# Window attention and two MLPs on one Trainium2 core: where layer two's pieces of x are formed, and in which banks the last half accumulates

## The chip, the core and the metric

One of the eight cores of a Trainium2 chip runs the whole program. Its engines work side by side, each through a queue of its own: TensorE (PE, its weight loads PEld) multiplies matrices, VectorE (DVE), ScalarE (ACT) and GpSimd (POOL) do the elementwise work, and SyncE (SP) issues the transfers (DMA). The metric is the device time of one execution in microseconds (us); less is better.

## The reference

Four sequences of 576 tokens, eight heads of 64, go through causal attention in a window of 64 tokens; the 2304 x 512 result goes through two MLPs with 2048 hidden units, the first with `s * relu(h)^2 + b`, the second with a leaky relu of its own slope for each unit.

```python
scores = scale * np.matmul(q, k.transpose(0, 1, 3, 2))
mask = (rel >= 0) & (rel < 64)
attn = softmax(np.where(mask, scores, -1e9))
x = np.matmul(attn, v)                                  # as 2304 x 512
r = np.maximum(x @ moe_w_in, 0.0)
x = (moe_s * (r * r) + moe_b) @ moe_w_out               # layer one
h = x @ moe2_w_in
out = (np.maximum(h, 0.0) + alpha * np.minimum(h, 0.0)) @ moe2_w_out   # layer two
```

## The kernel before

**Numbers in two parts.** Every operand of a large product is held as a high and a low part, hi + lo (`pair`, L667): hi is a cast (ScalarE, or VectorE at L671), lo the rest (a subtraction on VectorE, L674). A product is three matmuls: hi x hi, hi x lo, lo x hi.

**Tiling.** A hidden tile f is 128 of the 2048 hidden units; `GROUPS` splits the 16 tiles of a layer into groups whose projections are summed in PSUM, and the groups' sums are added up in AY in SBUF (`sums`, L1168). The first two groups of layer one work on blocks of tokens (`hidden`, L1058). All later groups take the tokens in three turns q of 768, each two halves c of 384 (`HALF`), and the hidden tiles in pairs. A pair by a turn is a 2 x 2 block product in seven products instead of eight (`hidden_pair`, L913; its matmuls are L939): seven combinations of x, the *pieces* 1 to 7, by seven of the weights, six matmuls of 384 columns each. With 48 matmuls of projections (`project`, L1096, at L1139) a pair by a turn is 90 matmuls. Layer two's groups have four tiles each, so two pairs: in each turn a piece is used twice.

**Banks of PSUM.** Products 1 and 5 begin in two banks of a ring of two (`b1`, `b4`, tag "h"), products 6, 7 and 3 run in the two halves of `hb`; ScalarE carries running sums from one to the next (L950: b1 to hb's first half, that to the second, that to b4), VectorE adds the product 5 to both halves of `hb` at once (L967). The hidden function's relus (L1035, L1036 in layer two, L1016 in layer one) read `b1`, `b4` and that sum; then come L1039, the cast to hi (L1004 on ScalarE, L1005 on VectorE) and the subtraction to lo (L1009). The projections accumulate in the four banks y0 to y3, one buffer each, over the tiles of a group; after a half's last tile VectorE adds each into AY (L1188; L1185 at the end of layer one; L1181 copies at the start of layer two), and the last group's sums go out (L1193).

**Pieces of x.** In layer two they are formed from AY by `x_pieces` (L869): pieces 1, 2 and 3 are blocks of x, 5, 6, 7 and 4 differences T1 to T4 (L882, two places in AS, each used twice a turn). `x_stage` puts hi and lo of a piece into AG with `staging` (L678), which has room for two pieces, and stores it in DRAM (`x_store`, L792). At a turn's start `x_load` (L901, its transfer L907) fetches the seven pieces into seven slots of XA; a slot is free when the second pair of the turn before has used it. A turn that follows itself at a group's boundary keeps its pieces. So layer two's first group loads three turns, the other three groups two each. `weight_pair` (L725) forms the weights' combinations for a pair ahead of time, through the same AG (L757) and DRAM; `weight_load` fetches them (L778). `weight` converts an output tile's weights (L639 to L674).

**Order of the work.** `T.step` registers a step with its possible engines, what it reads and writes, and a due time `at`; `T.emit` (L162) then plays all steps through with costs of its own and writes each engine's queue in that order: of the steps that can start first on an engine it takes the one with the earliest `at`. On the chip each queue runs in this order. `T.tile` and `T.place` make a step wait for the users of what it overwrites, in the order in which the steps were registered. `begin` holds when a turn should start, `PAIR` the planned time of a pair by a turn (15.4 us); products are due at begin + pair x `PAIR` + a seventh for each, a half's projections from 1.7 `PAIR` after begin on.

## Time and profile before

| | us |
|---|---|
| median of 3 runs | 862.49 (862.11 to 864.53) |
| the profiled execution | 862.62 |
| its span, first to last instruction | 860.9 |
| TensorE busy | 838.3 (97%) |
| VectorE busy | 650.4 (76%) |
| ScalarE busy | 511.2 (59%) |
| pieces loaded, `ax<-xd` | 112 transfers of 768 KB, 6.6 us each to land |
| pieces of layer two stored, `xd<-ag` | 21 transfers of 768 KB, 5.7 us each to land |

The page also cuts the span into 40 slices of 21.5 us. TensorE is busy nine tenths or more in all but the first and the last but one, the one from 495 to 516 us, which is also the only one in which its granted clock shows 8 tenths instead of 9 or more. Busy time of TensorE is modelled from pipelined matmuls; idle time and the distance of matmuls tell more than the share. Layer two's first group runs from about 461 to 561 us.

### The profile page before, as it was taken

Reading aid. Unit: us, or ns where it says so; the run is one execution under the profiler, and the core shown is the slowest. Engines: PE = TensorE matmul, PEld = TensorE weight load, DVE = VectorE, ACT = ScalarE, POOL = GpSimd, SP = SyncE. Lnnn points to the kernel's source line nnn. Section 1 sums busy time; section 2 is a strip of 40 time slices with the busy share of each in tenths; the row PEclk is TensorE's granted clock in tenths of the full one; section 3 lists DMA queues with packets and bytes.
Section 4 is the critical chain, followed back from the end, with each engine's and each line's share of the span. In section 5 each row is a group of like instructions: output and inputs, shape, how many; then the busy total and the mean of one; then the engine's idle time right before and its main releaser. Section 6 shows DMA issues by size and latency. Waiting matters only on the chain.

```text
span 860.9 us, 14923 instructions
## 1 busy us (share of the span) xinstructions
PE 838.3 (97%) x5556; PEld 790.3 (92%) x5556; DVE 650.4 (76%) x1175; ACT 511.2 (59%) x1217; POOL 104.2 (12%) x113
## 2 busy tenths in 40 slices
PE   7799999999999999999999989999999999999997
PEld 4678888888899999999999989999999999999997
DVE  6878798798987795699677986588676976864554
ACT  6878996555576574566554655576464655544431
POOL 6543354332110010010000000000000000000000
PEclk9999999999999999999999989999999999999999
DMA  8676884577478979957799979948774768425822
GB/s 282 201 204 190 286 229 131 184 238 292 166 270 338 388 248 371 353 197 304 288 374 394 386 303 347 339 150 327 279 271 135 249 265 321 144 102 192 294 74 74
DMA packets 68616, 219.09 MB, mean 255 GB/s; under 512 B 6976, under 2 KB 25408, under 8 KB 68544
## 3 DMA queue, kind: packets, MB, share of 16 engines
q1 hardware_dynamic: 68544, 218.14, 70.6%
q8 instruction: 44, 0.72, 0.3%
q14 instruction: 28, 0.23, 0.1%
HBM read 160.18 MB, written 57.93 MB: 253 GB/s over the span
## 4 chain that ended last, share of the span: by engine, by line
PE 77%; DMA 9%; DVE 7%; ACT 3%; POOL 2%; issue 1%; SPq 0%; POOLq 0%; ACTq 0%; DVEq 0%
PE y L1139 34%; PE h L939 16%; PE ab L939 13%; PE h L1069 5%; PE y L1121 4%; DMA xd<-aq 2%; DMA raw<-w_in 2%; PE y L604 2%; DMA ax<-xd 2%; PE y L573 2%; PE ab L499 1%; POOL as__89 L556 1%; DMA xd<-ag 1%; ACT as__89 L538 1%; DMA wd<-ag 1%
## 5 line engine op out<-in xcount | busy, mean ns | idle before, releaser
L1139 PE MATMUL y<-ax,woh 128*128 128x384 f32 x1248 | 284.0, 336 | 2.3 <-DVE ay L1188 0.8
L1139 PEld LDWEIGHTS y<-ax,woh 128*128 128x128 f32 x1248 | 222.6, 188 | 5.1 <-DVE ay L1188 2.0
L939 PE MATMUL h<-ax,aw 128*128 128x384 f32 x936 | 187.4, 336 | 0.8 <-ACT r L1016 0.6
L1139 PE MATMUL y<-ax,wol 128*128 128x384 f32 x624 | 174.2, 335 | 0.0
L939 PEld LDWEIGHTS h<-ax,aw 128*128 128x128 f32 x936 | 165.0, 189 | 2.6 <-ACT r L1016 1.2
L939 PE MATMUL ab<-ax,aw 128*128 128x384 f32 x702 | 141.6, 337 | 3.6 <-DMA ax<-xd 2.1
L939 PEld LDWEIGHTS ab<-ax,aw 128*128 128x128 f32 x702 | 123.9, 189 | 4.8 <-issue 2.4
L1139 PEld LDWEIGHTS y<-ax,wol 128*128 128x128 f32 x624 | 114.3, 188 | 0.0
L1188 DVE TENSOR_TENSOR ay<-y,ay 128x384 f32<-128x384 f32 x120 | 63.2, 553 | 44.7 <-PE y L1139 44.5
L1009 DVE TENSOR_TENSOR ax<-r,ax 128x384 fp32r<-128x384 f32 x156 | 86.2, 559 | 8.6 <-ACT ax L1004 6.6
L1069 PE MATMUL h<-ax,aw 128*128 128x512 f32 (+1 forms) x360 | 85.0, 380 | 0.8 <-DVE ax L622 0.6
L1069 PEld LDWEIGHTS h<-ax,aw 128*128 128x128 f32 x360 | 62.8, 192 | 12.8 <-DVE ax L622 1.0
L1039 DVE SCALAR_TENSOR_TENSOR r<-aq,nalpha,r 128x384 f32<-128x384 f32 x96 | 58.6, 613 | 16.8 <-ACT aq L1036 11.8
L967 DVE TENSOR_TENSOR aq<-ab,aq 128x768 f32<-128x768 f32 x39 | 37.3, 955 | 40.6 <-PE ab L939 39.0
L643 ACT ACTIVATE wt<-raw 128x512 f32<-128x512 f32 x64 | 43.1, 677 | 34.9 <-DMA raw<-w_out 14.0
L1004 ACT CAST ax<-r 128x384 fp32r<-128x384 f32 x83 | 42.5, 513 | 22.6 <-DVE r L1039 20.2
L1035 ACT ACTIVATE r<-aq 128x384 f32<-128x384 f32 x48 | 24.8, 518 | 45.7 <-DVE aq L967 45.7
L1020 ACT ACTIVATE r<-r 128x384 f32<-128x384 f32 (+2 forms) x90 | 47.5, 542 | 1.2
L556 POOL TENSOR_TENSOR as__89<-as__89,den 128x512 f32<-128x512 f32 x36 | 40.8, 1154 | 56.4 <-DVE den L549 43.7
L657 DVE SCALAR_TENSOR_TENSOR raw<-raw 128x512 int32<-128x512 int32 x64 | 47.1, 738 | 0.2 <-ACT raw L647 0.2
L647 ACT ACTIVATE raw<-raw 128x512 int32<-128x512 uint32 x64 | 42.7, 679 | 5.1 <-DMA raw<-w_in 3.8
L662 DVE CUSTOM_DVE_ANT_0 wt<-raw,wt 128x1024 uint16<-128x1024 uint16 x64 | 45.0, 706 | 0.3
(126 smaller groups left out, 1125.2 us busy)
## 6 DMA issues: line engine op xcount, KB each, us to landing
ax<-xd SPq DMA_DIRECT2D x112, 768.0 KB, 6.6
wd<-ag SPq DMA_DIRECT2D x33, 512.0 KB, 6.4
aw<-wd SPq DMA_DIRECT2D x33, 512.0 KB, 5.2
raw<-w_in SPq DMA_DIRECT2D x32, 512.0 KB, 5.1
raw<-w_out SPq DMA_DIRECT2D x32, 512.0 KB, 6.4
xd<-ag SPq DMA_DIRECT2D x21, 768.0 KB, 5.7
xd<-aq SPq DMA_DIRECT2D x12, 768.0 KB, 4.0
xd<-ax SPq DMA_DIRECT2D x36, 192.0 KB, 4.8
```

What stands on the lines that cost most here:

```text
L556: eng.tensor_mul(x, x, d)
L643: [act(512, lambda: nc.scalar.activation(T[t], H().bitcast(F32), AF.Abs, scale=65536.0))],
L647: [act(512, lambda: nc.scalar.activation(L(), L().bitcast(U32), AF.Copy, scale=2.0 ** -29))],
L657: [dve(512, lambda: nc.vector.scalar_tensor_tensor(out=L(), in0=H(), scalar=-0x80000000, in1=L(), op0=ALU.bitwise_and, op1=ALU.bitwise_or) ...
L662: [dve(512, lambda: nc.vector.tensor_tensor(ti(), ti(), L(), op=ALU.add), port=True)],
L939: nc.tensor.matmul(bank(), W[:, wj, a, kt * P:(kt + 1) * P], X[:, c, kt, :], start=start and kt == 0 and y == 0, stop=kt == 1 and y == 2, ...
L1009: [dve(n, lambda: nc.vector.tensor_sub(T[gl], rn(), f32(T[gh])), port=True)],
L1020: [act(n, lambda: nc.scalar.activation(rn(), rn(), AF.Square)), dve(n, lambda: nc.vector.tensor_mul(rn(), rn(), rn()), port=True)],
L1039: [dve(HALF, lambda: nc.vector.scalar_tensor_tensor(out=rn(), in0=r2n(), scalar=nalpha[:, f:f + 1], in1=rn(), op0=ALU.mult, op1=ALU.add), ...
L1069: nc.tensor.matmul(T[ps][:, :n].rearrange("p (c t) -> p c t", t=P), T[w][:, k * P:(k + 1) * P], T[X(x, k)], start=st, stop=sp,)
L1139: nc.tensor.matmul(ps, T[w][:, m * P:(m + 1) * P], T[x], start=(i == 0 and j == 0), stop=(last and j == 2),)
L1188: ways = [dve(n, lambda a=a, yn=yn: nc.vector.tensor_add(a(), yn(), a()))]
```

## The change

Layer two's pieces are no longer formed in staging slots. For its first group each piece is formed in the slot of XA that the group's products read (`x_slot`), and the store to DRAM leaves from there; the first group's 21 loads are gone, the other groups' loads stay. The steps of `x_pieces` are registered at each turn's start instead of after layer one's last turns; their due times go from begin - 25 for all to begin - 16 (`SOON`) plus a seventh of `PAIR` for each piece in the order of use. The weight pair that is converted during that group is registered after its turns instead of before. Apart from that, the last half of the last group accumulates its four output blocks in two buffers of the ring "h" (blocks 0 and 3) and in the two halves of `hb` (1 and 2), and no longer in y0 to y3.

```diff
--- before.py
+++ after.py
@@ -37,6 +37,7 @@
 W2 = 256
 GRING = 10
 LAG = 1.7
+SOON = 16.0
 PAIR_AT = (0, 3584)
 W_AT = (0, 1024, 2048, 3584, 4608, 5632)
 
@@ -794,10 +795,10 @@
             )
 
         def x_stage(layer, q, j, s, reads, at):
-            if layer == 0:
+            if layer == 1:
+                x = x_slot(layer, 0, q, j)
+            else:
                 x = T.place(f"XS{j}.{layer}.{q}", AQ, 0, XW, F32R)
-            else:
-                x = staging(f"XS{j}.{layer}.{q}", XW)
             key = f"{x}."
             T.parts[key + "h"] = T.parts[key + "l"] = x
             pair(C, s, lambda: x2(T[x][:, :C]), lambda: x2(T[x][:, C:]), reads, [key], at)
@@ -883,7 +884,7 @@
                 )
 
             def piece(j, s, reads):
-                x_stage(1, q, j, s, reads, at)
+                x_stage(1, q, j, s, reads, at + ORDER.index(j) * PAIR / 7)
 
             tv = lambda n: (lambda: x2(T[temps[n]]))
             piece(1, lambda: B(0, 0), src(0, 0))
@@ -898,9 +899,12 @@
             add(4, lambda: B(1, 0), tv(2), src(1, 0) + [temps[2]])
             piece(4, tv(4), [temps[4]])
 
+        def x_slot(layer, g, q, j):
+            x_load.slots[j] = T.place(f"X{j}.{layer}.{g}.{q}", XA, (j - 1) * XW, XW, F32R)
+            return x_load.slots[j]
+
         def x_load(layer, g, q, j, at):
-            x = T.place(f"X{j}.{layer}.{g}.{q}", XA, (j - 1) * XW, XW, F32R)
-            x_load.slots[j] = x
+            x = x_slot(layer, g, q, j)
             key = f"{x}."
             T.parts[key + "h"] = T.parts[key + "l"] = x
             T.step(
@@ -918,7 +922,9 @@
             slot = PAIR / 7
             if p == 0 and x_load.held != (layer, q):
                 x_load.held = (layer, q)
-                for j in ORDER:
+                if (layer, g) == (1, 0):
+                    x_pieces(q, begin[1, 0, q] - SOON)
+                for j in ORDER if (layer, g) != (1, 0) else ():
                     x_load(layer, g, q, j, begin[layer, g, q] - 10.0)
             b1 = T.tile("b1." + pr, h_ps, [P, 512], F32, "h", 2)
             b4 = T.tile("b4." + pr, h_ps, [P, 512], F32, "h", 2)
@@ -1093,6 +1099,14 @@
 
         hidden.n = 0
 
+        def closing(layer, g, pt):
+            return (layer, g) == order_of[-1] and pt == f"{2 * turns[layer, g][-1] + 1}"
+
+        def y_key(m, layer, g, pt):
+            if closing(layer, g, pt) and m in (1, 2):
+                return "hb", m - 1
+            return f"y{m}.{layer}.{g}.{pt}"
+
         def project(layer, g, part, i):
             fs = groups[layer][g]
             f = fs[i]
@@ -1107,7 +1121,7 @@
                 pt = f"{part}"
             wh, wl = f"w.{layer}.{f}.1h", f"w.{layer}.{f}.1l"
             gh, gl = f"gh{layer}.{pt}.{f}", f"gl{layer}.{pt}.{f}"
-            Y = lambda m: f"y{m}.{layer}.{g}.{pt}"
+            Y = lambda m: y_key(m, layer, g, pt)
             if (layer, g) == (0, 0):
 
                 if i == len(fs) - 1:
@@ -1128,7 +1142,12 @@
                 return
             if i == 0:
                 for m in range(NK):
-                    T.tile(Y(m), y_ps, [P, 512], F32, f"y{m}")
+                    if Y(m) in T.tiles:
+                        continue
+                    if closing(layer, g, pt):
+                        T.tile(Y(m), h_ps, [P, 512], F32, "h", 2)
+                    else:
+                        T.tile(Y(m), y_ps, [P, 512], F32, f"y{m}")
             passes = ((wh, gh), (wh, gl), (wl, gh))
             last = i == len(fs) - 1
 
@@ -1174,7 +1193,7 @@
                 if g == SPLIT[layer]:
                     T.place(acc, AY, m * NT + b0, n)
                 a = lambda acc=acc: T[acc]
-                y = f"y{m}.{layer}.{g}.{hf}"
+                y = y_key(m, layer, g, f"{hf}")
                 yn = lambda y=y: T[y][:, :n]
                 reads = [y]
                 if g == 0:
@@ -1235,6 +1254,8 @@
                         first_sum(g, bi, m)
 
         T.tile("hb", a_ps, [P, 2, 512], F32, "ab")
+        for x in range(2):
+            T.tiles["hb", x] = lambda x=x: T["hb"][:, x, :]
 
         def prime():
             wide = idle.rearrange("p (o c) -> p o c", o=1).to_broadcast([P, 4, P])
@@ -1261,11 +1282,16 @@
             for i, f in enumerate(fs):
                 at = t + LAG * PAIR + i * PAIR / 4 - 12.0 - 15.0 * end
                 weight(layer, f, 1, at, at - AHEAD)
-            for e in range(EARLY[x]):
-                layer_, g_, p_ = next(k for k, v in number.items() if v == early)
-                at = t + 25.0 + e * took / EARLY[x]
-                weight_pair(early, layer_, *groups[layer_][g_][2 * p_:2 * p_ + 2], at, at - 30.0, False)
-                early += 1
+            def ahead():
+                nonlocal early
+                for e in range(EARLY[x]):
+                    layer_, g_, p_ = next(k for k, v in number.items() if v == early)
+                    at = t + 25.0 + e * took / EARLY[x]
+                    weight_pair(early, layer_, *groups[layer_][g_][2 * p_:2 * p_ + 2], at, at - 30.0, False)
+                    early += 1
+
+            if (layer, g) != (1, 0):
+                ahead()
             for q in turns[layer, g]:
                 for p in range(len(fs) // 2):
                     hidden_pair(layer, g, q, p)
@@ -1275,8 +1301,8 @@
                     for i in range(len(fs)):
                         project(layer, g, 2 * q + c, i)
                     sums(layer, g, 2 * q + c)
-                if end:
-                    x_pieces(q, begin[1, 0, q] - 25.0)
+            if (layer, g) == (1, 0):
+                ahead()
         assert early == len(number)
         T.emit()
 
```

## Rows read from the trace of the kernel before

**Rows 1.** Waits of TensorE, 440 to 560 us (us in total, times, longest us):

```profile
PE ab L939 <- DMA ax<-xd: 2.1, 1, 2.1
PE ab L939 <- ACT h L950: 0.6, 1, 0.6
PE h L939 <- ACT r L1016: 0.6, 1, 0.6
PE h L939 <- DMA ax<-xd: 0.2, 1, 0.2
```

**Rows 2.** Waits of TensorE, 520 us to the end:

```profile
PE y L1139 <- DVE ax L1005: 0.5, 1, 0.5
```

**Rows 3.** Busy us (count) of engines, granted clock, DMA share, GB/s by windows:

```profile
500.00:510.00 10.00, 9.13 (x34) 8.56 (x35) 8.20 (x12) 4.71 (x10) 0.00 (x0) 0.66 0.80 326
```

**Rows 4.** Chain of waits, a piece after the stall (start us, us, what):

```profile
512.61 2.08 PE y L1139 x12
```

**Rows 5.** Timeline of TensorE, 496 to 509 us (start us, us, line, tiles, count):

```profile
496.92 1.21 PE L939 MATMUL h<-ax,aw 128*128 128x384 f32 x6
500.26 1.31 PE L939 MATMUL ab<-ax,aw 128*128 128x384 f32 x6 [2.13 <-DMA ax<-xd]
502.17 2.29 PE L939 MATMUL ab<-ax,aw 128*128 128x384 f32 x6 [0.61 <-ACT h L950]
...
508.63 0.33 PE L1139 MATMUL y<-ax,wol 128*128 128x384 f32 x1
```

**Rows 6.** DMA issues, 430 to 520 us (count, KB each, us to landing):

```profile
xd<-ag SPq DMA_DIRECT2D x16, 768.0 KB, 5.5
ax<-xd SPq DMA_DIRECT2D x16, 768.0 KB, 7.8
```

**Rows 7.** Timeline of SP's queue, 420 to 530 us:

```profile
459.59 2.30 SPq L778 DMA_DIRECT2D aw<-wd  x4
...
492.69 5.40 SPq L907 DMA_DIRECT2D ax<-xd  x4
```

**Rows 8.** Timeline of TensorE, second pair of turn one, first product of turn two:

```profile
477.16 1.20 PE L939 MATMUL h<-ax,aw 128*128 128x384 f32 x6
...
492.76 1.20 PE L939 MATMUL h<-ax,aw 128*128 128x384 f32 x6
```

**Rows 9.** L669, L671, L674, L882, 420 to 530 us (duration ns min/median/max, first and last start):

```profile
L669 ACT CAST ag<-ay x5: 821/837/839, 478.8 to 519.3; 128x768 fp32r<-128x768 f32 x5
...
L671 DVE CAST ag<-as__89 x6: 552/558/560, 423.1 to 523.5; 128x768 fp32r<-128x768 f32 x6
...
L674 DVE TENSOR_TENSOR ag<-ay,ag x8: 947/952/959, 436.4 to 520.4; 128x768 fp32r<-128x768 f32 x8
...
L882 DVE TENSOR_TENSOR as__89<-ay x6: 948/951/951, 422.1 to 508.0; 128x768 f32<-128x768 f32 x6
```

**Rows 10.** Busy us of engines by windows (PE, PEld, DVE, ACT, POOL; clock, DMA share):

```profile
445.00:474.00 29.00, 28.19 (x159) 27.17 (x158) 21.83 (x39) 14.05 (x29) 0.00 (x0) 1.00 1.00 384
478.00:503.00 25.00, 22.26 (x126) 21.64 (x125) 23.60 (x44) 15.78 (x33) 0.00 (x0) 0.97 1.00 385
```

**Rows 11.** Groups of VectorE, 478 to 503 us (busy us, mean ns, idle before):

```profile
L657 DVE SCALAR_TENSOR_TENSOR raw<-raw 128x512 int32<-128x512 int32 x3 | 2.1, 687 | 0.0
...
L652 DVE TENSOR_SCALAR wt<-wt 128x512 f32<-128x512 f32 x3 | 1.3, 420 | 0.0
```

**Rows 12.** Timelines of TensorE and VectorE, 843 to 847 us:

```profile
844.42 0.86 PE L1139 MATMUL y<-ax,wol 128*128 128x384 f32 x4
845.80 1.03 PE L1139 MATMUL y<-ax,woh 128*128 128x384 f32 x2 [0.52 <-DVE ax L1005]
...
846.85 0.52 PE L1139 MATMUL y<-ax,woh 128*128 128x384 f32 x2
...
845.78 0.56 DVE L1009 TENSOR_TENSOR ax<-r,ax 128x384 fp32r<-128x384 f32 x1
```

**Rows 13.** Waits of VectorE, 425 to 530 us:

```profile
DVE ag L671 <- DMA xd<-ag: 4.4, 4, 2.2
```

## The prediction

> **What bounds the kernel now.** First the list of TensorE's waits. In the stretch of layer two's first group, 440 to 560 us, it names four: 2.1 us for a transfer into `ax` (a piece of x), 0.6 for a copy of ScalarE behind it, 0.6 for a relu and 0.2 for another piece [rows 1]. From 520 us to the end it names one, 0.5 us for a cast [rows 2]. So TensorE sets the time nearly everywhere, and the change can gain only where it stands idle or runs slowly: around 500 us and at the end. Second, the table by windows: between 500 and 510 us the granted clock is 0.66 on the mean and 34 matmuls are counted [rows 3]; around it, 12 matmuls take 2.08 us, 0.173 us each [rows 4].
>
> Third, TensorE's timeline there [rows 5]. The six matmuls that start at 496.92 would end at 496.92 + 6 x 0.173 = 497.96. The next six start at 500.26, after idling 2.13 for `ax`, six more at 502.17 after 0.61 for the copy, and these and those after them come 0.34 us apart: the lower of the two clock levels, 1.2 GHz, reached after those two idle times. At 508.63 the pace is back. From 497.96 to 508.63, 10.67 us, 26 matmuls ran (18 of products in three sixes, 8 of projections); at 0.173 they need 4.50. **The stall costs 6.2 us**: 2.7 of waits, the rest mostly the 20 matmuls at half pace (20 x 0.17 = 3.4).
>
> Its cause is the round trip through DRAM. A piece of turn two is cast and subtracted into one of two staging slots in AG, stored (5.5 us to land), then loaded into its slot in XA (7.8) [rows 6]; the two staging slots are filled again only when the stores have left them. The last four loads of turn two go out from 492.69 [rows 7], the very time its first product starts (492.76 in [rows 8]); TensorE's wait ends at 500.26, 7.6 us after the first of them.
>
> **The change part by part.** *(a) The 21 loads of the first group go* (7 pieces x 3 turns, 768 KB each), and the 21 stores stay, read from the XA slots. What ends last before a product is no more store plus load (5.5 + 7.8) but the forming alone: hi on ScalarE 0.84 (or VectorE 0.56), lo on VectorE 0.95 [rows 9], so 1.5 to 1.8 us and two hand-overs. The DMA engines are full from 478 to 503 (share 1.00) [rows 10]; 21 x 0.79 = 16.5 MB less at 385 GB/s is 43 us of their time. It sets no time of its own afterwards.
>
> *(b) The forming moves behind the products.* Piece j of turn two can be written only when the second pair of turn one has used slot j. The first such product starts at 477.16 and turn two's first product at 492.76 [rows 8]. A product takes 6 x 0.173 = 1.04, so a piece has 492.76 - 477.16 - 1.04 = 14.6 us, and since turn two's products follow in the same order this holds for each of the seven. 1.8 us fit in easily if the engines have room. VectorE: busy 23.60 of 25 us from 478 to 503 [rows 10]. In that are 7.8 us of pieces by today's schedule (five subtractions at 0.95, two casts at 0.55, two differences at 0.95, by [rows 9]), so 15.8 of other work. The new turn needs seven lo at 0.95 (6.7), the two differences that can't run ahead (1.9), and two or three casts (1.1 to 1.7): 9.7 to 10.3, in all 25.5 to 26.1 of 25 us. But the three weight conversions in the window (four steps each, L657 to L652, two of them 2.1 us for the three and two 1.3 [rows 11]; 6.8, 2.3 each) are, two of the three, those of the weight pair that is due 25 us into the group and used only in the next; put off they leave 21 of 25. In turn one's window, 445 to 474, VectorE was busy 21.8 of 29 [rows 10], 7.2 of it pieces (four lo, one cast, three differences), and takes 12 instead: 27 of 29. Full, not over. ScalarE, 15.8 of 25 [rows 10], takes four casts there already and would take at most three more (2.5).
>
> *(c) Waits added.* Each first write of a piece now waits for a product. Queued behind it on ScalarE or VectorE are the copies that TensorE's next product needs, and the halves for the projections. Bounds: nothing, and 6.2 us for one stall as large as today's. The row that it is nearest to is the 0.6 us wait for a relu [rows 1], since the planner knows the length of engine work and is out with transfers above all; I take one of 0.6 and one of 0.2, **+0.8**. On SP the 21 stores wait for their lo as they did in staging; behind them stand weight loads. Those of the group's second pair were issued at 459.59 [rows 7]; at the 7.8 us of a load here they land at 467.4, some 10 us before they are used (477.16). That covers what SP is held up; without it, it would be paid one for one.
>
> *(d) Edits at nothing.* The weight pair that is emitted after the turns keeps its due time. Its sums stand in the place of the differences T1 and T3, and were behind turn three's before too; it is used a whole pair into the next group, two turns later at least (31 us). Layer two's first sums overwrite AY columns that the pieces read: a turn's sums come about two pairs after its forming. The small wait for `ax` of 0.2 [rows 1] goes with the loads: **-0.2**.
>
> *(e) The last half in other banks.* Near the end 4 matmuls start at 844.42 and would end at 845.12. The next three start at 845.80, after 0.52 for a cast, and the fourth only at 846.85, when the lo of the same half has come (VectorE, 845.78 plus 0.56) [rows 12]. Three matmuls need 0.52, so 846.85 - 845.12 - 0.52 = **1.2 us** are lost. They belong to the first-to-last half, whose last hidden block is the last product. The last half's first twelve matmuls (2.08 us) need only old halves, but the same four banks. In the banks of the last pair (`b1`, the two of `hb`, and `b4`, which is wanted last and is read before that subtraction) these can stand in the gap. Bounds 0 (the order stays) and 1.2; the twelve are longer than the gap, so I take all of it. The sums and the output after the last matmul stay.
>
> Sum against the profiled execution's own 862.62 (span 860.9, 1.7 around it; 0.13 above the median 862.49): 862.62 - 6.2 - 0.2 - 1.2 + 0.8 = **855.8**.
>
> **The rivals.** *One stall is left.* The forming in one turn comes late enough for TensorE to idle. For it: VectorE's 25.5 to 26.1 of 25 us if the conversions aren't put off. Against: only the last pieces would be late, and projections stand between. Price 2.7 (waits alone) to 6.2 (with the clock): 858.5 to 862.0.
>
> *Nothing comes of it.* The stall's place is taken by one as large, and the tail's order stays: 862 to 862.6.
>
> *Slower: a cast at the head of an engine's queue.* Where the planner puts a cast too early, its engine stands before a slot that TensorE has not released, with the copies and halves that TensorE needs behind it. Such waits are in the trace: VectorE's casts idled 4.4 us in four times for a store [rows 13], and TensorE's list shows no wait that came of it [rows 1]. The Trainium skill ("TensorE: Matmul & The Clock Gate", section "Architectural detail: the array is 16× 32×32, not 1× 128×128") calls the queues of ScalarE and VectorE strictly first in, first out, which would pass each such wait on to all that is behind; the trace's casts behave so, and by the rule the sum would be this rival's, by the row zero. Now the thing awaited is TensorE itself, so a wait can feed back. It decides from the point where a piece's wait and the work behind it exceed the 14.6 us. If two of three turns stall as today's one does: 855.8 + 2 x 6.2 = 868.2.
>
> **How the numbers follow.** Forecast 0.60 (854 to 858), one stall left 0.17, nothing 0.08, slower 0.15. The low end is the sum with no new wait and the relu's 0.6 gone too: 862.6 - 6.2 - 0.2 - 1.2 - 0.6 = 854.4, less 0.4 for the spread between runs: 854.0. The high end takes in the stall that is left and half of the third case, 862.4. About 0.3% (2.6 us: under 859.9, over 865.1) is what a measurement here can tell from no change. Faster: 0.60 and half of 0.17, 0.69; same: the other half and 0.08, 0.16; slower 0.15.
>
> **What would show it.** Right: no wait of TensorE for `ax<-xd` in layer two's first group, granted clock 1.00 in every 10 us window from 450 to 520, the DMA share there under 0.8, 91 loads `ax<-xd` in place of 112, no gap at the end between the first-to-last half's passes. Wrong: waits of L939 for the cast or the subtraction of a piece, or a window with a clock below 1; for (e), the wait for L1005 still there. What would make the prediction wrong: VectorE's conversions of the far weight pair ahead of the pieces in turn two, or a reordering of the later groups, where TensorE has no slack to lose.

## The result, and the profile after

| | before | after |
|---|---|---|
| median | 862.95 us (862.11 to 864.53, 4 runs) | 853.76 us (851.91 to 854.42, 4 runs) |
| profiled execution (span) | 862.62 (860.9) | 854.11 (852.3) |
| ratio, 95% interval | | 0.9888 (0.9866 to 0.991) |

The time fell by 9.2 us in the medians and by 8.5 in the profiled executions; 6.8 were forecast, and the range ended at 854.0, 0.2 above the median. The direction held; the gain was taken too small. The four executions of after lie 2.5 us apart, and the profiled one, 854.11, is just inside the range.

The page of after: the engines (busy time, share, instructions), and the bytes moved.

```profile
PE 832.7 (98%) x5556; PEld 787.7 (92%) x5556; DVE 651.1 (76%) x1175; ACT 510.5 (60%) x1217; POOL 103.5 (12%) x113
...
DMA packets 65592, 202.57 MB, mean 238 GB/s; under 512 B 6640, under 2 KB 25072, under 8 KB 65520
...
ax<-xd SPq DMA_DIRECT2D x91, 768.0 KB, 6.9
...
xd<-ax SPq DMA_DIRECT2D x21, 768.0 KB, 4.3
```

The 21 loads are gone (91 in place of 112), with 16.5 MB (219.09 before). A store of a piece lands in 4.3 us where it took 5.7. The list of TensorE's waits from 430 to 560 us, which had the four of [rows 1] and one of 0.2 for a sum, is empty. The table by windows of after (matmul counts in brackets behind PE; then VectorE and ScalarE, granted clock, DMA share, GB/s), and under it the same of before for four stretches:

```profile
440.00:460.00 20.00, 20.00 (x117) 20.00 (x116) 18.12 (x32) 11.95 (x24) 0.00 (x0) 1.00 0.80 283
460.00:480.00 20.00, 20.00 (x118) 20.00 (x117) 18.18 (x32) 11.51 (x25) 0.00 (x0) 1.00 0.50 190
480.00:500.00 20.00, 20.00 (x117) 20.00 (x116) 19.32 (x34) 14.64 (x31) 0.00 (x0) 1.00 0.51 209
500.00:510.00 10.00, 10.00 (x60) 10.00 (x59) 7.87 (x12) 5.10 (x11) 0.00 (x0) 1.00 0.68 274
...
445.00:474.00 29.00, 29.00 (x169) 29.00 (x168) 25.66 (x43) 15.83 (x32) 0.00 (x0) 1.00 0.78 289
478.00:503.00 25.00, 25.00 (x146) 25.00 (x145) 23.51 (x39) 17.68 (x36) 0.00 (x0) 1.00 0.55 224
```

```profile
440.00:460.00 20.00, 19.35 (x110) 18.65 (x109) 17.05 (x30) 10.41 (x21) 0.00 (x0) 1.00 1.00 377
460.00:480.00 20.00, 19.84 (x115) 19.52 (x114) 13.87 (x26) 10.40 (x23) 0.00 (x0) 1.00 0.98 377
480.00:500.00 20.00, 18.12 (x105) 17.80 (x103) 18.60 (x35) 12.94 (x26) 0.00 (x0) 1.00 1.00 384
500.00:520.00 20.00, 19.14 (x92) 18.56 (x93) 16.66 (x27) 11.43 (x24) 0.00 (x0) 0.83 0.75 295
```

After has 117 or 118 matmuls in every 20 us, and 60 between 500 and 510, where [rows 3] has 34 at a clock of 0.66. The full DMA of [rows 10] is down to 0.78 and 0.55 (in steps of 10 us it still reaches 0.87 from 450 to 460 and 0.95 from 460 to 470), with VectorE at 25.66 of 29 and 23.51 of 25. Before also falls short between 440 and 460, at a clock of 1.00: 110 instead of 117.

**Where the time went.** Both programs have 5556 matmul records, so the start of the k-th in one trace can be set against the k-th in the other. How far after is ahead, in us:

| stretch (time in before) | change | what lies there |
|---|---|---|
| up to 434 | -0.1 | layer one; on the way between -0.2 and +0.7 |
| 434 to 468 | +2.2 | small losses in turn one of the first group |
| 489 to 516 | +6.2 | the stall of turn two |
| 516 to 547 | +0.15 | |
| 630 to 641 | +0.5 | a loss in before's trace |
| 641 to 651 | -1.0 | a loss in after's trace |
| 651 to 839 | +0.1 | |
| 839 to the last matmul | +1.2 | the last halves |
| behind the last matmul | -0.7 | VectorE's last sums (0.4) and what follows them |

The sum is 8.5, the difference of the two executions. The two losses between 630 and 651 belong to these executions and not to the change: the trace of e2, which has before's code there, lacks the first, and those of e1, e5 and e6, which have after's, lack the second. The tail of after: TensorE's timeline where the last half takes the other banks (`h` and `ab` in place of `y`), then VectorE's at the end, with idle time and its releaser in brackets.

```profile
836.42 0.85 PE L1158 MATMUL y<-ax,wol 128*128 128x384 f32 x4
837.11 0.51 PE L1158 MATMUL h<-ax,woh 128*128 128x384 f32 x2
...
837.63 0.51 PE L1158 MATMUL ab<-ax,woh 128*128 128x384 f32 x2
...
839.19 0.51 PE L1158 MATMUL y<-ax,woh 128*128 128x384 f32 x2
```

```profile
847.19 1.02 DVE L1207 TENSOR_TENSOR ay<-ab,ay 128x384 f32<-128x384 f32 x2 [0.48 <-PE ab L1158]
848.13 0.55 DVE L1207 TENSOR_TENSOR ay<-h,ay 128x384 f32<-128x384 f32 x1
```

Four matmuls start at 836.42 and end their pace at 837.11; the twelve of the last half fill 837.11 to 839.19, and the first-to-last half goes on in `y` without the gap of [rows 12]. At the very end VectorE idles 0.48 for `ab`: the tile `hb` is one tile of two banks, and the sum of its first half waits until the second half is written.

### The profile page after: what moved, and what is told of

The parts are those of the page before. It is cut to its first block, busy times and chain, and to the rows that moved or that the text cites. A ratio compares the mean times of both kernels' runs of the same rounds, so it can differ in the third digit from the quotient of the medians.

```text
span 852.3 us, 14883 instructions
## 1 busy us (share of the span) xinstructions
PE 832.7 (98%) x5556; PEld 787.7 (92%) x5556; DVE 651.1 (76%) x1175; ACT 510.5 (60%) x1217; POOL 103.5 (12%) x113
## 4 chain that ended last, share of the span: by engine, by line
PE 88%; DMA 5%; ACT 2%; POOL 2%; DVE 1%; issue 1%; SPq 0%; DVEq 0%; POOLq 0%; ACTq 0%
PE y L1158 38%; PE h L945 18%; PE ab L945 13%; PE h L1075 9%; PE y L1135 4%; PE y L605 2%; DMA wd<-ag 2%; DMA raw<-w_out 2%; PE y L574 2%; PE ab L500 1%; DMA raw<-w_in 1%; POOL as__89 L557 1%; ACT as__89 L539 1%; PE ab L1158 0%; PE h L1158 0%
## 5 line engine op out<-in xcount | busy, mean ns | idle before, releaser
L1158 PE MATMUL y<-ax,woh 128*128 128x384 f32 x1216 | 275.4, 334 | 0.4 <-DVE ay L1207 0.4
L1158 PEld LDWEIGHTS y<-ax,woh 128*128 128x128 f32 x1216 | 216.3, 188 | 1.2 <-DVE ay L1207 0.9
L945 PE MATMUL h<-ax,aw 128*128 128x384 f32 x936 | 185.3, 335 | 0.3 <-ACT r L1022 0.2
L1158 PE MATMUL y<-ax,wol 128*128 128x384 f32 x608 | 169.4, 334 | 0.0
L945 PEld LDWEIGHTS h<-ax,aw 128*128 128x128 f32 x936 | 164.2, 188 | 1.4 <-ACT r L1022 0.6
L945 PE MATMUL ab<-ax,aw 128*128 128x384 f32 x702 | 140.4, 335 | 2.0 <-ACT h L956 1.5
L945 PEld LDWEIGHTS ab<-ax,aw 128*128 128x128 f32 x702 | 123.1, 188 | 2.9 <-ACT h L956 1.8
L1158 PEld LDWEIGHTS y<-ax,wol 128*128 128x128 f32 x608 | 111.1, 188 | 0.0
L1207 DVE TENSOR_TENSOR ay<-y,ay 128x384 f32<-128x384 f32 x116 | 60.3, 552 | 38.5 <-PE y L1158 38.4
L973 DVE TENSOR_TENSOR aq<-ab,aq 128x768 f32<-128x768 f32 x39 | 37.3, 956 | 31.1 <-PE ab L945 29.1
```

Source lines behind the costliest of these rows:

```text
L945: nc.tensor.matmul(bank(), W[:, wj, a, kt * P:(kt + 1) * P], X[:, c, kt, :], start=start and kt == 0 and y == 0, stop=kt == 1 and y == 2, ...
L1158: nc.tensor.matmul(ps, T[w][:, m * P:(m + 1) * P], T[x], start=(i == 0 and j == 0), stop=(last and j == 2),)
L1207: ways = [dve(n, lambda a=a, yn=yn: nc.vector.tensor_add(a(), yn(), a()))]
```

## The experiments

Each ratio is to the kernel before, run beside it on the same chip. "Loss" is matmuls missing at 0.173 us each, or the shift between two traces' k-th matmuls.

| kernel | median us (runs) | ratio, 95% interval |
|---|---|---|
| e1_slots_only | 854.48 (4) | 0.989 (0.9853 to 0.9927) |
| e2_tail_only | 862.21 (12) | 0.9995 (0.9975 to 1.0014) |
| e4_three_staging | 867.76 (10) | 1.0059 (1.0037 to 1.0082) |
| e9_loads_unchained | 862.51 (10) | 1.0001 (0.9974 to 1.0028) |
| e12_half_transfers | 857.30 (7) | 0.9929 (0.9901 to 0.9957) |
| e3_idle_loads | 922.35 (4) | 1.0682 (1.0649 to 1.0716) |
| e3b_idle_loads | 859.27 (10) | 0.9974 (0.9954 to 0.9995) |
| e10_idle_loads_pool | 870.11 (4) | 1.0089 (1.0059 to 1.012) |
| e5_lo_twice | 864.87 (10) | 1.0032 (1.0012 to 1.0052) |
| e6_pair_first | 866.91 (4) | 1.0064 (1.004 to 1.0088) |
| e8_hb_first | 854.50 (6) | 0.9907 (0.9876 to 0.9938) |
| e11_raw_earlier | 856.00 (6) | 0.9925 (0.9898 to 0.9951) |

### The two parts alone

The slots alone: the changed kernel with the last half back in its four banks.

```diff
-            return (layer, g) == order_of[-1] and pt == f"{2 * turns[layer, g][-1] + 1}"
+            return False
```

> The changed kernel with the last half back in y0 to y3. Theory A (the loads' round trip and the two staging slots are the whole loss in layer two's first group, the banks a loss of their own at the end): no wait of TensorE between 430 and 560 us, clock 1.00 there, the gap of 1.2 us near the end back, the median 1.2 us above the changed kernel's 853.8, so about 855.0. Rival (the two parts help each other through the planner's order): a gap at the end other than 1.2, or waits in the first group.

The shifts between 434 and 516 us are those of after to the hundredth (+2.2 and +6.2), and at the end TensorE's list has the wait of 0.5 for the cast of the first-to-last half again, and one of 0.2 for its lo.

The banks alone, in the kernel before (`closing`, `y_key`, the tiles `hb`, as in the change):

```diff
+        def closing(layer, g, pt):
+            return (layer, g) == order_of[-1] and pt == f"{2 * turns[layer, g][-1] + 1}"
...
-            Y = lambda m: f"y{m}.{layer}.{g}.{pt}"
+            Y = lambda m: y_key(m, layer, g, pt)
```

> The kernel before with only the last half's banks moved. Theory A: the stall at 498 to 508 us stays (6.2 us), the gap near the end goes; 1.2 us less at TensorE's last matmul, less what comes after it: about 862.0 against 863.0. If the sums after the last matmul end later relative to it, as the changed kernel's do (its span ends 4.6 us after the last matmul, before 4.0), 0.6 of that is lost: 862.3.

The last halves take 1.2 us less than before's, the term (e), but the time cannot be told from none. In the medians the slots alone give 7.6 of the 9.2 us. By the traces alone the banks gain 1.2 at TensorE and lose 0.5 (e2) to 0.7 (after) behind the last matmul. e2 also has the first group of before unchanged, and its stall between 489 and 516 us is 4.4 us by the shifts: the 6.2 are those of one execution.

### What made the stall: the round trip, the slots or the traffic

The prediction's cause was the round trip: two staging slots, a store, then a load that waits for it. The rival is the traffic: DMA engines so full that every transfer lands late. First the slots: AG widened, so that a third staging slot fits.

```diff
-    AG = area("ag", 2 * GH * NMAX)
+    AG = area("ag", 2 * GH * NMAX + 512)
```

> The kernel before with AG wider by 512 columns, so that three pieces can be staged instead of two. Theory A (two staging slots, each taken until its store has left, pace the round trip and make VectorE and ScalarE stand in front of them): the casts' waits for stores (VectorE 4.4 us, ScalarE 5.3 between 425 and 530) fall by half or more, the last four loads of turn two go out some us before 492.7, the wait of 2.1 at 500 goes or shrinks below the point where the clock falls; gain 3 to 8 us, 855 to 860. Rival (the transfers alone, at a share of 1.00, are too slow): the stall stays, 862 to 863.

It became slower, outside both expectations. TensorE's waits from 430 to 560, VectorE's from 428 to 472, and three windows:

```profile
PE ab L939 <- DMA ax<-xd: 5.5, 3, 2.3
PE h L939 <- DMA ax<-xd: 3.4, 1, 3.4
...
DVE ag L671 <- DMA xd<-ag: 8.7, 3, 3.7
...
430.00:450.00 20.00, 19.82 (x115) 19.42 (x114) 10.75 (x20) 9.94 (x20) 0.00 (x0) 1.00 0.96 354
450.00:470.00 20.00, 20.00 (x117) 19.85 (x116) 13.78 (x22) 9.29 (x18) 0.00 (x0) 1.00 1.02 414
...
490.00:510.00 20.00, 14.18 (x67) 13.60 (x68) 17.17 (x34) 9.93 (x21) 0.00 (x0) 0.86 0.71 276
```

The small losses of turn one are gone nearly (115 and 117), but the stall of turn two has grown, and turn three has one too (84 matmuls from 530 to 550): transfers into `ax` still come late with more slots to stage in. That does not clear the slots, since the planner also put other transfers ahead of the loads. From 470 to 512 us SP stands 12.2 us, up to 4.9 at a time, before raw weight tiles whose place VectorE still reads (L639), with loads of pieces behind in its queue. The three loads that TensorE waits for there left behind such tiles, and then took 6.6 to 9.3 us to land.

Then the order: in the kernel before, the first group's loads read layer one's pieces, which lie in DRAM since long. The traffic stays, and no load waits for a store to land.

```diff
-                dma(1, P * XW * 4, lambda: nc.sync.dma_start(out=f32(T[x]), in_=xd[layer * NQ + q, j - 1])),
-                reads=[f"xd.{layer}.{q}.{j}"], writes=[key + "h", key + "l"], at=at,
+                dma(1, P * XW * 4, lambda: nc.sync.dma_start(out=f32(T[x]), in_=xd[(layer if g else 0) * NQ + q, j - 1])),
+                reads=[f"xd.{layer if g else 0}.{q}.{j}"], writes=[key + "h", key + "l"], at=at,
```

> The kernel before, with the first group's 21 loads reading layer one's pieces, long in DRAM, in place of the pieces just stored: all transfers stay, but no load waits for a forming or a store (layer two then works on other data in its first group). Theory A: the last four loads of turn two no longer wait at 492.7 for stores, the stall at 498 to 508 goes; the small waits of 430 to 470 (2.2 us by the count of matmuls) stay, since pieces are staged as before: 6 us less than before, about 856.5. Rival B (a share of 1.00 is too much by itself): the loads land as late as before, the stall stays, 861 to 863.

Nothing is won: 862.51. Its profiled execution, at 859.07 one of the quicker ones, has a smaller stall than [rows 1] and waits for the loads still, with the DMA engines full:

```profile
PE ab L939 <- DMA ax<-xd: 1.0, 1, 1.0
...
470.00:490.00 20.00, 20.00 (x118) 20.00 (x117) 16.92 (x30) 12.01 (x24) 0.00 (x0) 1.00 0.99 387
490.00:510.00 20.00, 17.91 (x100) 16.99 (x100) 19.90 (x35) 13.92 (x29) 0.00 (x0) 1.00 0.87 348
```

17 of 117 matmuls are missing there (2.9 us). But the edit frees the loads only half. In SP's queue they stand behind the same stores as before, and SP stands before these stores until VectorE has formed the lo. SP's queue and its waits, 470 to 512 us, in before and then in e9:

```profile
490.04 2.52 SPq L792 DMA_DIRECT2D xd<-ag  x2
492.69 5.40 SPq L907 DMA_DIRECT2D ax<-xd  x4
...
SPq L792 <- DVE ag L674: 29.1, 7, 7.3
SPq L907 <- DMA xd<-ag: 3.4, 2, 2.8
```

```profile
489.70 2.52 SPq L792 DMA_DIRECT2D xd<-ag  x2
492.63 3.06 SPq L907 DMA_DIRECT2D ax<-xd  x4
...
SPq L792 <- DVE ag L674: 30.2, 8, 7.3
```

The load that ends the wait of 2.13 (turn two's fourth) leaves at 492.69 in before and at 492.63 in e9. In before it lands at 500.12, 7.4 us later, and the product could have started at 497.96: both leaving late and landing slowly made it late. The fifth waited 2.8 for a store to land and left at 496.30, 2.7 us before 499.00, when its product could have followed (an estimate by the 1.04 us of a product); in before no transfer of 768 KB that left between 470 and 512 us lands in less than 3.2, so after that wait it could not be on time. The store itself had taken 5.9 us to land. In e9 that wait is gone, and the last three loads leave 2.5 to 3.2 us sooner. So e9 shows that the waits for landed stores are not the whole cause; it does not clear the round trip.

Then the traffic: in the kernel before, only the hi half of each of layer two's pieces is stored, and loaded again in the first group. The order of store and load, and the staging slots, stay; 42 transfers are 0.39 MB smaller, 16.5 MB together, as much as the change removes. The planner is told the smaller size too.

```diff
+            H = XW if layer == 0 else C
-                dma(1, P * XW * 4, lambda: nc.sync.dma_start(out=xd[layer * NQ + q, j - 1], in_=f32(T[x]))),
+                dma(1, P * H * 4, lambda: nc.sync.dma_start(out=xd[layer * NQ + q, j - 1, :, :H], in_=f32(T[x])[:, :H])),
...
+            H = C if (layer, g) == (1, 0) else XW
```

> The kernel before, with only the hi half of each piece of layer two stored, and loaded for the first group (21 stores and 21 loads of 384 KB instead of 768; the later groups fetch their lo halves from layer one's pieces, so layer two's result is not the reference's). The chain of staging, store and load stays; 42 x 0.39 = 16.5 MB go, as many as the change takes away. Theory C (the full DMA engines are the cost, the chain is only where it reaches TensorE): the stall at 500 goes, the small waits for staging slots may stay: 855 to 858. Theory A (the chain itself is too long): each of its two transfers is about 1 us shorter, the stall shrinks by 2 to 3 at most: 859 to 862.

Four windows, and of SP's queue and its waits from 470 to 512 us the last four loads of turn two:

```profile
430.00:450.00 20.00, 19.06 (x107) 18.05 (x106) 15.79 (x29) 13.27 (x27) 0.00 (x0) 1.00 0.91 322
450.00:470.00 20.00, 19.27 (x112) 18.95 (x111) 17.34 (x31) 11.05 (x22) 0.00 (x0) 1.00 0.94 355
470.00:490.00 20.00, 20.00 (x117) 20.00 (x116) 18.14 (x33) 10.76 (x23) 0.00 (x0) 1.00 0.49 159
490.00:510.00 20.00, 20.00 (x117) 20.00 (x116) 18.51 (x30) 13.95 (x31) 0.00 (x0) 1.00 0.34 119
...
483.04 7.54 SPq L910 DMA_DIRECT2D ax<-xd  x4
...
SPq L910 <- PE h L947: 14.5, 4, 7.8
```

857.30, 5.5 us under the kernel before. The stall is gone whole, though each piece is still stored and then loaded, and DMA has room from 470 on. But more than the bytes is different: turn two's seven loads now leave within 0.3 us of the product that last used their slots, the last four from 483.04 to 490.26 instead of 492.69 to 497.77, because no store that waits for its lo stands before them. So e12 takes away the late leaving and the slow landing together, and which of the two ended the stall isn't shown.

The losses of turn one are all there (107 and 112 of 117). In these runs they go with the staging slots: they are in before, here, in e2 and in e9, all with two slots; 1.6 of the 2.2 are gone in e4 with three, all in e1, after and e3b with none.

By which wait the slots cost them isn't shown. The casts stand before full slots in before (3.7 us on VectorE and 1.9 on ScalarE from 428 to 472), but in e4, where TensorE lost little, they stood longer (8.7 and 4.0).

### The traffic put back into the changed kernel

21 loads of 768 KB that nobody reads go into the staging slots of the changed kernel, which only the weight pairs still use. The first form gave them a latest time only:

```diff
                     x_pieces(q, begin[1, 0, q] - SOON)
+                    for j in ORDER:
+                        d = staging(f"D{j}.{q}", XW)
+                        T.step(
+                            dma(1, P * XW * 4, lambda d=d, j=j: nc.sync.dma_start(out=f32(T[d]), in_=xd[q, j - 1])),
+                            reads=[f"xd.0.{q}.{j}"], writes=[f"{d}.d"], at=begin[1, 0, q] - 10.0,
+                        )
+                        T.parts[f"{d}.d"] = d
```

> The changed kernel with 21 loads of 768 KB put back at the due times of those that went, from layer one's pieces in DRAM into the staging slots, where nobody reads them. Theory A (the round trip was the cost, not the traffic): DMA share back to about 1.0 between 440 and 520, no wait of TensorE there, 853.8 within 1. Rival B (the transfers that are left only became quick enough because the traffic fell): waits for weights or for stores' slots return, 2.7 to 6.2 us, 856.5 to 860.

The planner sent them in layer one, into columns that layer one's halves use; some 68 us went there ("PE y L1142 <- DMA ag<-xd: 26.7, 7, 5.2" heads TensorE's list from 80 to 320 us). It says nothing of the first group. With an earliest time as well:

```diff
-                            reads=[f"xd.0.{q}.{j}"], writes=[f"{d}.d"], at=begin[1, 0, q] - 10.0,
+                            reads=[f"xd.0.{q}.{j}"], writes=[f"{d}.d"],
+                            at=begin[1, 0, q] - 10.0, after=begin[1, 0, q] - 10.0,
```

> The changed kernel with 21 loads of 768 KB put back, 10 us ahead of each turn of layer two's first group and not earlier, from layer one's pieces in DRAM into the staging slots, where nobody reads them. Theory A (the chain of forming, store and load was the cost): DMA share up to 0.9 or 1.0 between 450 and 520, no wait of TensorE there for more than 0.5, 853.8 within 1.5. Rival B (full DMA engines are the cost, whatever hangs on them): waits of 2.7 to 6.2 us return, for weights above all, 856.5 to 860.

859.27: 5.5 of the 9.2 us are given back in the medians (3.6 between the two traces) by transfers that nobody reads. TensorE's waits from 430 to 560, and windows:

```profile
PE h L953 <- DMA aw<-wd: 0.8, 1, 0.8
PE h L953 <- DVE ax L675: 0.8, 1, 0.8
...
450.00:470.00 20.00, 20.00 (x117) 20.00 (x116) 18.38 (x31) 9.29 (x18) 0.00 (x0) 1.00 1.01 388
470.00:490.00 20.00, 18.93 (x108) 18.22 (x107) 15.74 (x27) 12.20 (x24) 0.00 (x0) 1.00 1.00 394
```

There is no one large stall, but many small ones; from 450 to 490 the DMA engines are full, and from 490 to 510 as well (0.99), where 113 matmuls ran at a clock of 1.00 and before has 81. So engines as full as before's need not make the large stall where no piece makes the round trip; this is one of the quicker executions, 857.75, and those up to 864.60 have no trace. Stores of pieces land in 8.4 us from 430 to 520 where after has 4.1, the weights `aw<-wd` in 10.2 where after has 4.9. TensorE idles for a weight, for a lo, for a copy. Something does wait for the idle loads, though: from 425 to 560 us SP stands 37.3 us before the slots of those still on their way, with stores and weight loads behind, and two casts of the weight pair stand 6.1.

Is it the DMA engines, or SP's queue, in which the idle loads stand before the weights? The same loads issued by GpSimd:

```diff
-                            dma(1, P * XW * 4, lambda d=d, j=j: nc.sync.dma_start(out=f32(T[d]), in_=xd[q, j - 1])),
+                            [("pool", 1.0, lambda d=d, j=j: nc.gpsimd.dma_start(out=f32(T[d]), in_=xd[q, j - 1]), 4.0)],
```

> The changed kernel with the same 21 idle loads of layer one's pieces into the staging slots, now issued by GpSimd, which has nothing else to do there, instead of SP. Theory C (full DMA engines delay the transfers that TensorE needs): as with SP's queue, waits of some tenths for weights and pieces, 857 to 860. Rival (the cost with SP was its queue, which stood 37 us in front of the idle loads' slots with stores and weight loads behind): no such waits, within 1.5 of 853.8.

870.11, outside both expectations. One window of the trace, TensorE's waits in its part up to 450, ScalarE's and VectorE's behind them (425 to 470), and the raw weights in the table of issues (425 to 520):

```profile
430.00:450.00 20.00, 10.88 (x49) 9.72 (x48) 6.49 (x13) 5.59 (x11) 2.65 (x5) 0.84 1.02 414
...
PE y L1166 <- DVE ay L1212: 4.8, 2, 4.4
PE ab L953 <- ACT ab L964: 4.3, 1, 4.3
...
ACT wt L644 <- DMA raw<-w_out: 15.8, 3, 8.6
...
DVE wt L653 <- ACT wt L644: 8.3, 1, 8.3
...
raw<-w_out SPq DMA_DIRECT2D x4, 512.0 KB, 18.3
```

Raw weight tiles took 18.3 us to land, the median of four (6.4 over the whole of after). ScalarE stood before their conversion, VectorE behind ScalarE, and the copy and the sum that TensorE wanted stood behind both; 68 matmuls (12 us) are missing in these 20 us. SP's queue held none of the idle loads, and the cost was there: other transfers on the DMA engines are enough to make it. The Trainium skill ("DMA: Bandwidth & Descriptors", section "Issuing engines are not separate DMA queues") says that DMAs of every issuing engine run on the same 16 DMA engines and interleave; that agrees. 870.11 against 859.27 does not compare the two queues: with nothing before them in GpSimd's, the idle loads leave from 404.80 us on, in SP's from 434.18, so e10 also fills the end of layer one, where the 12 us are lost. How much of e3b's 5.5 is SP's queue stays open.

### The cover that the prediction leaned on

VectorE's room: the lo of each of layer two's pieces formed twice, seven more subtractions a turn (6.7 us of VectorE).

```diff
+            if layer == 1:
+                T.step(
+                    [dve(C, lambda: nc.vector.tensor_sub(x2(T[x][:, C:]), s(), f32(x2(T[x][:, :C]))), port=True)],
+                    reads=reads + [key + "h"], writes=[key + "l"], at=at,
+                )
```

> The changed kernel with the lo of each piece of layer two formed twice over, 0.95 us more of VectorE for each, 6.7 in a turn. By the room that the prediction counted (21 of 25 us in turn two with the far conversions put off) this is 27.7 of 25: pieces late, one or two stalls of 2.7 to 6.2, 857 to 866. Rival (VectorE has more room than that, since its work can move by a turn): no wait over 0.5 in the first group, within 1.5 of 853.8.

```profile
PE ab L950 <- DVE ax L807: 5.7, 1, 5.7
...
490.00:510.00 20.00, 12.34 (x56) 10.88 (x55) 19.34 (x32) 8.81 (x17) 0.00 (x0) 0.79 0.49 202
```

One stall, where part (b) had put the limit, in turn two, at 19.34 of 20 us of VectorE and half a DMA load. 61 matmuls are missing in the window (10.6 us), and the median is 11.1 above after's. The margin of (b) is real and smaller than 6.7 us.

The weight pair emitted ahead of the turns again, part (d):

```diff
-            if (layer, g) != (1, 0):
-                ahead()
+            ahead()
...
-            if (layer, g) == (1, 0):
-                ahead()
```

> The changed kernel with the weight pair of the first group registered ahead of the turns again. Its sums share AS with the differences T1 and T3, so turn one's pieces 5 and 7 then come behind them, and those can't start before 13 us ahead of the turn. Theory: piece 5 of turn one is late by some 5 to 12 us, a stall of that size and half clock behind it, 860 to 870; the price of the cover in (d). Rival: the conversions get done in the time that is left, within 1.5 of 853.8.

```profile
PE h L945 <- ACT ax L670: 6.0, 1, 6.0
...
470.00:490.00 20.00, 13.15 (x61) 12.09 (x61) 18.00 (x31) 7.36 (x12) 0.00 (x0) 0.83 0.42 170
```

TensorE waits 6.0 us for the cast of a difference. It is the expectation's theory and not the third rival's: no slot of TensorE's is awaited, but the cast (482.20) stands for its difference, which VectorE forms at 481.21, behind the weight pair's sums and casts (477.87 to 481.3). 56 matmuls are missing in the window (9.7 us), and the median is 13.2 above after. So the rank that the emission gives the pair's conversions behind the pieces is worth more than the whole change; without it the change would have been a loss.

### Two tries for more

The tile `hb` for blocks 0 and 1, which are summed first, and raw weights due 14 us ahead in place of 8:

```diff
-            if closing(layer, g, pt) and m in (1, 2):
-                return "hb", m - 1
+            if closing(layer, g, pt) and m in (0, 1):
+                return "hb", m
```

> The changed kernel with the last half's blocks 0 and 1, not 1 and 2, in the two halves of hb. In the changed kernel VectorE's sum of block 1 waits until block 2, in the same tile, is done too (0.48 us idle), and VectorE ends 1.0 us after TensorE instead of 0.6. With 0 and 1 there the wait moves ahead of four sums that then run without a gap: 0 to 0.5 us less, 853.3 to 853.8; no more than the spread of the runs can show. Rival: the sums start 0.5 later and end as late: no difference.

```diff
-writes=[(raw, 0), (raw, 1)], at=at - 8, after=after - 8,
+writes=[(raw, 0), (raw, 1)], at=at - 14, after=after - 14,
```

> The changed kernel with every raw weight tile's load due 14 us ahead of its conversion instead of 8. At 340 to 365 us ScalarE stands 3.4 us in front of a raw tile with the copy that TensorE waits 1.5 us for behind it, with the DMA share at 1.0. Theory: engines stand in front of late transfers, so earlier ones give back up to 2.5 us there: 851 to 854. Rival (where the DMA engines are full, an earlier load only makes another one late): 853 to 857.

Neither beats the changed kernel: 854.50 cannot be told from it, and 856.00 is no better. In the first, the first sum waits for both banks of the tile (VectorE idles 4.6 before it, 4.1 in after). In the second, TensorE wins 1.9 us around 350 us and loses 1.8 around 240 and 1.2 around 300; that other work comes later for the earlier loads is likely, and not shown.

## Why the prediction was right in its sign and too small

**Right.** The stall: the forecast said 6.2, the k-th matmuls say 3.2 + 3.0 = 6.2, waits and half-clock matmuls together; the clock is 1.00 in each window from 440 to 510. The last halves: 1.2 and 1.2 at TensorE. The loads, the clock and the list of waits came out as listed under what would show it; the DMA share, which was to be under 0.8 throughout, did not (0.95 from 460 to 470). VectorE was full and not over in turn two, but at 23.51 of 25 where (b) left 21, and e5 shows the limit of it. In turn one the sum of (b) gave 27 of 29, the trace 25.66.

**Mis-sized: the small waits.** This is the term that failed. The prediction took 0.2 for them, the wait for `ax` of [rows 1], and 0.6 more for the relu at the low end of its range. The shifts give 2.2 between 434 and 468. The list of waits names about half of what is lost. Before's timeline of TensorE:

```profile
444.27 1.20 PE L939 MATMUL h<-ax,aw 128*128 128x384 f32 x6
446.04 0.79 PE L939 MATMUL h<-ax,aw 128*128 128x384 f32 x3 [0.57 <-ACT r L1016]
```

Six matmuls at 444.27 need 1.04 and would end at 445.31; the next start at 446.04, 0.73 later, of which 0.57 is listed. The count by windows shows the loss whole: in before 110 and 115 matmuls from 440 to 480 where after has 117 and 118. The prediction had such a count: [rows 10] has 159 matmuls in 29 us, where 0.173 us each makes room for 168, but it took only VectorE, ScalarE and DMA from those rows.

**Open: the cause of the stall.** The prediction named the round trip, worked out in (a) that 43 us of DMA time go, and gave those no worth beside it. Before's trace has the round trip in it: loads behind stores that wait for their lo, and two loads that wait for a store to land. But the decisive load also took 7.4 us at a DMA share of 1.00. e9 shows that the waits for landed stores are not all of it, e12 that leaving on time with half the bytes ends the stall, e3b's trace that full engines without the round trip need not make it. No run keeps the late leaving and empties the engines, or the reverse. What e10 and e3b do show is that transfers nobody reads have a price here, which (a) left out. The number 6.2 came out whichever it was, as taking the loads away ends both.

**Wrong: the +0.8 for new waits.** In the first group there are none on TensorE. The casts do wait for slots, as the rival of the casts said they would; ScalarE's waits in after from 425 to 530:

```profile
ACT ax L670 <- PE ab L945: 5.3, 3, 2.7
...
ACT ax L670 <- PE h L945: 1.5, 3, 1.1
```

VectorE has four such, 2.5 us together, at most 1.1. The longest is 2.7; in e10 ScalarE stood up to 8.6 before a raw tile. The Trainium skill's rule on the strict queues of ScalarE and VectorE ("TensorE: Matmul & The Clock Gate", section "Architectural detail: the array is 16× 32×32, not 1× 128×128") holds in e10, where the copies behind the tile came late; in after no wait of TensorE followed from the shorter ones. That what stood behind had time left is the likely reason, and not shown. A loss of 1.0 appears instead at 635 us, of which the list has "PE ab L945 <- ACT ab L956: 0.5, 1, 0.5"; it is this execution's, and what makes it was not found.

**SP's cover.** It held, but was smaller than the 10 us of (c). In before the four weight loads of turn one's second pair [rows 7] took 10.2 to 12.2 us each and not 7.8; the last landed at 473.68, 3.5 us before the pair's first product (477.16). In after, where SP stands before the stores of the pieces for up to 13.4 us, they go out from 450.34 to 463.99; the last lands at 471.37, and the product starts at 475.11.

**The sum.** 6.2 + 2.2 + 1.2 + 0.15 + 0.5 + 0.1, less 1.0, 0.7 and 0.1, is 8.5, against 6.8. The 0.7 at the end stood in the prediction as "The sums and the output after the last matmul stay". With 2.2 for the small waits and without the +0.8 the sum would have been 853.0, below the 854.11 measured, mostly by what was lost at 635 and at the end.

## What to carry to other kernels

Count matmuls by window and compare with the pace: the list of waits gave 1.0 us between 430 and 470 where 2.2 were lost. When a transfer comes late, take apart when it left its queue and how long it took to land; and when an experiment is to change one of the two, compare the times at which the transfers left, since the planner may have changed the other (e4, e12) or the queue may have kept it (e9). And when work moves from a transfer onto an engine that is 94% busy, its rank against the other work there decides: the same change with one weight pair emitted earlier is 4 us slower than no change.

## What the runs showed of the hardware

- At a DMA share of 0.98 to 1.02 the core moved 377 to 414 GB/s in these windows. In e3b, 768 KB stores of pieces took 8.4 us to land and 512 KB weights 10.2, against 4.1 and 4.9 at the lower load of after, in the same stretch of 430 to 520.
- SP's queue passes a wait on: in e9 a load whose data lay ready left at 492.63, behind stores that stood for VectorE, as in before at 492.69.
- The stall of the kernel before isn't the same size in each execution: 6.2 us in before's trace, 4.4 in e2's, and 857.5 to 868.1 over 66 executions; what sets it was not found.
- Beside 768 KB loads issued by GpSimd, which landed in 8.1 us, raw weight tiles of 512 KB on SP's queue took 18.3 (e10, 425 to 520 us).
